# Moving the loads of batch 1's k and q, and their phi, among the steps of an attention-and-FFN kernel's first block

## The chip, the cores and the metric

The kernel runs on one core of a Trainium2 chip. The metric is device time in microseconds (us) of one execution; a "run" below is one execution. Traces are of one execution each, taken by the hardware profiler.

## The reference, cut to what matters

Cosine-weighted linear attention over 8 batches (8 heads, 576 positions, head width 64), then an RMS norm and a gated FFN (512 to 1536 to 512) on the 4608 tokens.

```python
def phi(x, c, s):                       # c, s: cosine and sine of the position
    r = np.maximum(x, 0.0)
    return np.concatenate([r * c, r * s], axis=-1)
q_p, k_p = phi(q, cos_w, sin_w), phi(k, cos_w, sin_w)
kv  = np.einsum('bhsf,bhsd->bhfd', k_p, v)
z   = np.sum(k_p, axis=2)
num = np.einsum('bhsf,bhfd->bhsd', q_p, kv)
den = np.einsum('bhsf,bhf->bhs', q_p, z)[..., None] + 1e-06
x   = num / den                         # then tokens by 512
xn  = x / rms(x) * rms_g
out = (silu(xn @ w_gate) * (xn @ w_val)) @ w_out
```

## The kernel before

The FFN goes block by block (512 tokens, one batch). A block has twelve gate steps, each with four matmuls by w_gate into a psG bank and four by w_val into a psV bank, and then the products with w_out. While PE (TensorE) works on a block's FFN, ACT (ScalarE) and DVE (VectorE) prepare the attention of the next batch. Each engine takes its own instructions in the order of the program, as every timeline here shows, so a wait holds up all that stands behind it (after the change, the sg of step 8, whose psG was ready near 34.3 us, ran at 36.98, behind two phis that had waited for k until 36.17). A bank is one of the buffers that PE writes its sums to; PE can fill it again only when ACT or DVE has read it. The order is written by hand:

```python
def phi(eng, out_ap, in_ap, scale):     # half of a phi: cosine on DVE, sine on ACT
    if eng is nc.scalar:
        nc.scalar.activation(out=out_ap, in_=in_ap, func=AF.Relu, scale=scale)
    else:
        eng.tensor_scalar(out=out_ap, in0=in_ap, scalar1=scale, scalar2=0.0,
                          op0=ALU.mult, op1=ALU.max)
# k_phi(eng, b, j, half) writes kpm from rk; q_phi(eng, b, c, half) writes qp from rq
...
def gval_step(blk, n, bank=None):
    bank = n % 2 if bank is None else bank       # two psG and two psV banks, taken in turn
    run(blk, n, "pe")
    gval_mm(blk, n, bank)                        # PE:  psG, psV
    run(blk, n, "pre")
    sg = gval_act(blk, n, bank)                  # ACT: sg = silu(psG)
    gval_h(blk, n, bank, sg)                     # DVE: hT = psV * sg
    run(blk, n, "post")                          # what at(blk, n, "post", ...) put there
...
# weight slices, issued from GpSimd (they cast to bf16), in this order:
#   0 to 5: w_gate and w_val, columns 0 to 768 in three pairs
#   6 w_gate, 7 w_val: columns 768 to 1152;  8 w_gate, 9 w_val: columns 1152 to 1536
#   then the first quarter of w_out
...
d = load_kv("k", 1)                              # issued from SP, as q and v
tc.add_manual_dep(d.ins, weight_dmas[7].ins.name, SYNC_DEP, reason="after the weights")
gate_q = load_q(1)
load_kv("v", 1, *LOW)
load_kv("v", 1, *HIGH)
w = wo_load(1)                                   # second quarter of w_out
tc.add_manual_dep(w.ins, gate_q.ins.name, SYNC_DEP, reason="after q of batch 1")
...
for j in range(NJ):                              # NJ = 9
    at(0, 8 + j // 4, "post", k_phi, V, 1, j, 0)
    at(0, 8 + j // 4, "post", k_phi, A, 1, j, 1)
for c in range(2):
    at(0, 10 + c, "post", q_phi, V, 1, c, 0)
    at(0, 10 + c, "post", q_phi, A, 1, c, 1)
...
for n in range(6, NNT):
    gval_step(0, n)                              # gate steps 6 to 11 of the first block
banks0 = [psC[0][:, :], psC[1][:, :], psG[0][:, :], psG[1][:, :]]
for n in range(NNT - 2):                         # w_out steps of the first block
    if n == 3:
        kvz_pe(1, psA)                           # "kvz": k_p^T [v, 1] of batch 1
        ...
    if 1 <= n <= 4:
        q_tr_pe(1, n - 1, qbank[n - 1])          # PE transposes q's phi, column n - 1
        ...
    if n == 0:
        for c in (2, 3):
            q_phi(V, 1, c, 0)
            q_phi(A, 1, c, 1)
    if n == 1:
        v_cast(A, 1, *LOW)
        v_cast(V, 1, *HIGH)
    ...
    for j in range(4):
        out_mm(0, j, n, banks0[j])
```

In the profile, L426 is gval_mm, L435 is sg, L441 is hT, L446 is out_mm, L209 is phi on ACT, L211 phi on DVE, L254 q_tr_pe, L282 kvz, L263 and L265 copies and casts on ACT and DVE, L79 and L90 the loads. rk, rq and rv are k, q and v as loaded; kpm and qp are what phi makes of k and q; vvm is v cast for kvz; rk<-in_k_dram is a load.

## Time and profile before

| | before |
|---|---|
| time | 328.86 us median (328.62 to 330.48, 3 runs) |
| span of the traced run | 327.9 us |
| PE busy | 318.9 us, 97% |
| PE's waits between gate step 6 and kvz | 0.25 and 1.03 us |

PE is the bound engine, so only its waits matter. First the part "busy us (share of the span) x instructions" of the page of the kernel before:

```profile
PE 318.9 (97%) x2441; PEld 161.0 (49%) x2441; DVE 185.9 (57%) x412; ACT 176.5 (54%) x366; POOL 32.1 (10%) x67
```

The timeline of PE before (start, length, engine, line, operation, what it writes and reads, count, and in brackets the idle time before it and who ended it):

```profile
39.64 1.02 PE L426 MATMUL psG<-xnT,wg 128*128 128x512 bf16 x4 [0.25 <-ACT sg L435]
...
43.20 0.38 PE L446 MATMUL psG<-wo,hT 128*128 128x512 bf16 x1 [1.03 <-ACT sg L435]
...
46.13 1.33 PE L282 MATMUL psA<-vvm,kpm 64*128 64x65 bf16 x72
```

PE waits for sg twice: gate step 11 wants the psG bank that the sg of step 9 has to empty, and the fourth w_out matmul wants the bank of step 11. The third line is kvz. ACT's timeline of the same stretch says why sg is late:

```profile
37.40 1.71 ACT L209 ACTIVATE kpm<-rk,tab 128x256 bf16<-128x256 f32 x4 [1.70 <-DMA rk<-in_k_dram]
39.01 0.57 ACT L435 ACTIVATE sg<-psG 128x512 f32<-128x512 f32 x1
39.49 1.69 ACT L209 ACTIVATE kpm<-rk,tab 128x256 bf16<-128x256 f32 x4
41.08 0.58 ACT L435 ACTIVATE sg<-psG 128x512 f32<-128x512 f32 x1
41.56 0.50 ACT L209 ACTIVATE kpm<-rk,tab 128x256 bf16<-128x256 f32 x1
41.96 0.71 ACT L209 ACTIVATE qp<-rq,tab 128x512 bf16<-128x512 f32 x1
42.57 0.58 ACT L435 ACTIVATE sg<-psG 128x512 f32<-128x512 f32 x1
```

ACT stands idle for 1.70 us until k has landed and then has no pause. SP's timeline has the issue of k, q and v:

```profile
27.46 0.38 SPq L79 DMA_DIRECT2D rk<-in_k_dram  x1
28.03 0.37 SPq L90 DMA_DIRECT2D rq<-in_q_dram  x1
28.57 5.19 SPq L79 DMA_DIRECT2D rv<-in_v_dram  x2
```

### The profile page before, as it was taken

To read this page: it belongs to the slowest core of one execution; us is meant where nothing else is said; L and a number is where in the kernel's file an instruction comes from. 1 tells how busy PE (TensorE), PEld (TensorE's weight loads), DVE (VectorE), ACT (ScalarE), POOL (GpSimd) and SP (SyncE) were. 2 spreads that over 40 slices of the span, in tenths; PEclk is the share of its full clock that TensorE was granted. 3 is DMA by queue.
4 is the path that set the end of the run, shared out by engine and by line. 5 is a ranking of instruction groups with operands and counts; after the bars stand their busy time and mean duration, and the time that the engine had idled before them with its cause. 6 is when DMAs were issued, how large, how long until landed. Compare 5 with 4: busy or idle time off the path is not lost.

```text
span 327.9 us, 6438 instructions
## 1 busy us (share of the span) xinstructions
PE 318.9 (97%) x2441; PEld 161.0 (49%) x2441; DVE 185.9 (57%) x412; ACT 176.5 (54%) x366; POOL 32.1 (10%) x67
## 2 busy tenths in 40 slices
PE   7999989999999999999999999999999999999994
PEld 2488455654445444544454445444544444444442
DVE  6775577777755875578257745773577133203310
ACT  6864575875566457645654576456644233223321
POOL 1660022001100110011001100110011000000000
PEclk9999999999999999999999999999999999999999
DMA  7999999998969866975598569957621400020014
GB/s 260 217 186 224 371 165 333 325 172 198 252 187 171 209 185 170 222 206 159 186 222 193 148 187 224 197 166 210 130 49 32 130 32 0 28 102 1 0 34 96
DMA packets 80337, 53.91 MB, mean 164 GB/s; under 512 B 51377, under 2 KB 67761, under 8 KB 80306
## 3 DMA queue, kind: packets, MB, share of 16 engines
q1 hardware_dynamic: 73264, 48.64, 57.8%
q0 software_dynamic: 6880, 4.72, 10.0%
q8 instruction: 19, 0.31, 0.4%
q10 hardware_dynamic: 162, 0.13, 0.2%
q14 instruction: 12, 0.10, 0.1%
HBM read 37.75 MB, written 9.44 MB: 144 GB/s over the span
## 4 chain that ended last, share of the span: by engine, by line
PE 83%; DMA 8%; ACT 4%; DVE 1%; issue 1%; SPq 1%; POOL 0%; ACTq 0%
PE psC L446 26%; PE psG L426 24%; PE psV L426 24%; DMA rk<-in_k_dram 3%; PE psA L282 3%; DMA wv<-in_moe_w_val_dram 3%; DMA rv<-in_v_dram 2%; PE psA L310 2%; ACT kpm L209 2%; PE psG L446 1%; ACT sg L435 1%; PE psC L826 1%; PE psV L254 1%; ACT qp L209 0%; PE psA L317 0%
## 5 line engine op out<-in xcount | busy, mean ns | idle before, releaser
L441 DVE TENSOR_TENSOR hT<-psV,sg 128x512 bf16<-128x512 f32 x102 | 70.3, 689 | 97.4 <-PE psV L426 84.9
L435 ACT ACTIVATE sg<-psG 128x512 f32<-128x512 f32 x102 | 60.6, 594 | 65.9 <-PE psG L426 65.8
L426 PE MATMUL psG<-xnT,wg 128*128 128x512 bf16 (+1 forms) x368 | 92.9, 375 | 0.3 <-ACT sg L435 0.2
L426 PE MATMUL psV<-xnT,wv 128*128 128x512 bf16 (+1 forms) x368 | 92.7, 374 | 0.0
L446 PE MATMUL psC<-wo,hT 128*128 128x512 bf16 x396 | 89.6, 379 | 0.0
L426 PEld LDWEIGHTS <-wv 128*128 128x128 bf16 x416 | 40.7, 98 | 47.4
L446 PEld LDWEIGHTS <-hT 128*128 128x128 bf16 x420 | 40.2, 98 | 46.4
L426 PEld LDWEIGHTS <-wg 128*128 128x128 bf16 x416 | 38.6, 98 | 41.7 <-issue 0.5
L263 ACT COPY osb<-psC 128x512 f32<-128x512 f32 (+1 forms) x33 | 19.2, 582 | 41.0 <-PE psC L446 39.7
L380 POOL TENSOR_TENSOR rs<-ms,mhalf 128x1 f32<-128x1 f32 x36 | 19.9, 551 | 200.2 <-ACT scr L375 200.2
L387 DVE SCALAR_TENSOR_TENSOR xn<-xt,rs,gb 128x512 bf16<-128x512 f32 x36 | 26.8, 745 | 14.7 <-POOL rs L380 14.7
L375 ACT ACTIVATE scr<-xt 128x513 bf16<-128x513 f32 x36 | 22.9, 635 | 21.4 <-DVE xt L364 21.2
L209 ACT ACTIVATE kpm<-rk,tab 128x256 bf16<-128x256 f32 (+1 forms) x78 | 31.8, 477 | 3.5 <-DMA rk<-in_k_dram 3.5
L364 DVE TENSOR_TENSOR xt<-psA,rec 128x512 f32<-128x512 f32 x35 | 24.2, 691 | 1.2
L211 DVE TENSOR_SCALAR kpm<-rk,tab 128x256 bf16<-128x256 f32 (+1 forms) x84 | 22.1, 329 | 3.0 <-DMA rk<-in_k_dram 3.0
L209 ACT ACTIVATE qp<-rq,tab 128x512 bf16<-128x512 f32 x32 | 22.5, 714 | 0.2 <-DMA rq<-in_q_dram 0.2
L211 DVE TENSOR_SCALAR qp<-rq,tab 128x512 bf16<-128x512 f32 x32 | 15.1, 484 | 0.5 <-DMA rq<-in_q_dram 0.5
L310 PEld LDWEIGHTS <-qpT 128*128 128x128 bf16 x248 | 11.6, 98 | 6.7 <-issue 0.3
L310 PE MATMUL psA<-kvzs,qpT 128*128 128x65 bf16 x248 | 12.8, 194 | 0.2
L426 PE MATMUL psV<-xnt_tail,wv 128*128 128x512 bf16 x48 | 12.3, 379 | 0.0
L426 PE MATMUL psG<-xnt_tail,wg 128*128 128x512 bf16 x48 | 12.3, 379 | 0.0
L282 PEld LDWEIGHTS <-kpm 64*128 64x128 bf16 x576 | 9.9, 95 | 3.8 <-issue 2.7
(89 smaller groups left out, 168.4 us busy)
## 6 DMA issues: line engine op xcount, KB each, us to landing
out_dram<-osb SPq DMA_DIRECT2D x32, 256.0 KB, 2.5
rv<-in_v_dram SPq DMA_DIRECT2D x21, 288.0 KB, 3.2
rk<-in_k_dram SPq DMA_DIRECT2D x20, 288.0 KB, 3.5
rq<-in_q_dram SPq DMA_DIRECT2D x20, 256.0 KB, 3.4
rk<-in_k_dram SPq DMA_DIRECT2D x2, 1152.0 KB, 8.8
rq<-in_q_dram SPq DMA_DIRECT2D x2, 1024.0 KB, 11.4
rv<-in_v_dram SPq DMA_DIRECT2D x3, 576.0 KB, 10.4
wo<-in_moe_w_out_dram POOLq DMA_DIRECT2D x4, 384.0 KB, 7.0
```

The costliest lines, as they stand in the source:

```text
L209: nc.scalar.activation(out=out_ap, in_=in_ap, func=AF.Relu, scale=scale)
L211: eng.tensor_scalar(out=out_ap, in0=in_ap, scalar1=scale, scalar2=0.0, op0=ALU.mult, op1=ALU.max)
L282: nc.tensor.matmul(banks[c][:, r * E : (r + 1) * E], lhsT=kp_main[b][lo : lo + 64, j, r, :], rhs=vvm[b % 2][lo : lo + 64, r, j, :], start= ...
L310: nc.tensor.matmul(o[:, g, i, :], lhsT=qpT[(b, 0)][:, h, j * P : (j + 1) * P], rhs=kvz_of(b, h), start=True, stop=True,)
L364: nc.vector.tensor_tensor(out=xt[:, 0:DM].rearrange("p (b h d) -> p b h d", b=2, d=D), in0=o[:, :, :, 0:D], in1=rec[:, :, :].unsqueeze(3). ...
L375: nc.scalar.activation(out=scr[:, :], in_=xt[:, 0 : DM + 1], func=AF.Square, scale=1.0 / math.sqrt(DM), accum_out=ms[:, :],)
L380: nc.gpsimd.tensor_tensor(out=rs[:, :], in0=ms[:, :], in1=mhalf[:, :], op=ALU.pow)
L387: nc.vector.scalar_tensor_tensor(out=xn[:, :], in0=x_of[(b, j)][:, 0:DM], scalar=rs_of[(b, j)][:, :], in1=gb[:, :], op0=ALU.mult, op1=ALU. ...
L426: nc.tensor.matmul(pst[bank][:, cols[0] : cols[1]], lhsT=w[:, t, n * P : (n + 1) * P], rhs=x[:, t, cols[0] : cols[1]], start=(t == 0), sto ...
L435: nc.scalar.activation(out=sg[:, :], in_=psG[bank][:, :], func=AF.Silu)
L441: nc.vector.tensor_tensor(out=hTs[blk][:, n, :], in0=psV[bank][:, :], in1=sg[:, :], op=ALU.mult)
L446: nc.tensor.matmul(bank, lhsT=hTs[blk][:, n, j * P : (j + 1) * P], rhs=wo[:, n, :], start=(n == 0), stop=(n == NNT - 1),)
```

## The change

Its intent: k arrives earlier, ahead of the last weight slices, and its phi comes in twos instead of fours, so that sg is never far behind. q goes behind the last gate slice so that it does not compete with it. The whole change:

```diff
     d = load_kv("k", 1)
-    tc.add_manual_dep(d.ins, weight_dmas[7].ins.name, SYNC_DEP, reason="after the weights")
+    tc.add_manual_dep(d.ins, weight_dmas[6].ins.name, SYNC_DEP, reason="after most weights")
     gate_q = load_q(1)
+    tc.add_manual_dep(
+        gate_q.ins, weight_dmas[8].ins.name, SYNC_DEP, reason="after the gate weights"
+    )
 ...
     for j in range(NJ):
-        at(0, 8 + j // 4, "post", k_phi, V, 1, j, 0)
-        at(0, 8 + j // 4, "post", k_phi, A, 1, j, 1)
-    for c in range(2):
-        at(0, 10 + c, "post", q_phi, V, 1, c, 0)
-        at(0, 10 + c, "post", q_phi, A, 1, c, 1)
+        at(0, 7 + j // 2, "post", k_phi, V, 1, j, 0)
+        at(0, 7 + j // 2, "post", k_phi, A, 1, j, 1)
+    at(0, 11, "post", q_phi, V, 1, 0, 0)
+    at(0, 11, "post", q_phi, A, 1, 0, 1)
 ...
         if n == 0:
-            for c in (2, 3):
+            for c in (1, 2, 3):
                 q_phi(V, 1, c, 0)
                 q_phi(A, 1, c, 1)
```

No instruction is added or taken away.

## The prediction

> **What bounds the kernel.** TensorE: the page gives PE busy for 318.9 of 327.9 us (97%), at full granted clock. In the waits view PE's named waits sum to under 5 us, and two of them lie where the change acts, both on ACT's Silu (sg): 0.25 us at 39.6 us (gate step 11) and 1.03 us at 43.2 us (a w_out matmul that takes over the bank of step 11). ACT's timeline has the cause. k of batch 1 is issued at 27.46 us, when weight slice 7 lands, and lands at 37.4. ACT, in program order, waits 1.70 us for it, then does phi four at a time (1.7 us) ahead of the sg of steps 10 and 11. So at most 1.28 us (0.4%) is to be had.
>
> **What changes.** No instruction is added or removed; PE's order is the same. k waits for one slice less: by the landings it is issued near 25.5 us. q waits for the last gate slice (landed 29.4 before), so near 29.6 instead of 28.03; v queues behind it.
>
> **DMA.** By the packets, k first flowed at 31.0 us, 3.5 us after its issue (1.1 us at the start of the kernel); until then the weights alone wrote about 200 GB/s. From 31.0 both flowed, weights at 100 and k at 200, which agrees with the round robin that the Trainium skill describes (DMA: Bandwidth & Descriptors, Queues, rings and completion order). Estimate from these: k flows from about 29 us and, at 200 GB/s for 1.18 MB, lands near 35 (34 to 36). The last weight slice slips from 31.2 to about 33; PE wants it at 36.6. q follows k without a gap and lands near 39.8 (40.2 before), v near 42 and 43.5.
>
> **After.** ACT reaches the first phi behind the sg of step 7, at 34.0, and waits about 1 us. Then two phis (0.9 us) and one sg (0.5 us) fit each 1.73 us step, so ACT catches up by step 10, and the sg of step 11 ends near 40.9, before PE wants the bank (41.8). Both waits go: 1.28 us. Some may be handed back: three q phis and the cast of v now stand directly before kvz on an ACT without slack (cast ends near 44.9, when PE arrives): 0 to 0.4 us. w_out's second part, still issued after q (landed 45.8), is wanted at about 46.3: 0 to 0.3 us. Later stages only shift.
>
> **Predicted:** 328.86 - 1.3 + 0.2 = 327.8 us, range 326.9 to 329.0. Faster by over 2%: 0.01; within 2%: 0.98; slower by over 2%: 0.01.
>
> **What would show it.** Right: k's packets start near 29 us; ACT waits for rk at 34, about 1 us; PE's waits at 39.6 and 43.2 are gone; kvz of batch 1 (46.2 before) starts near 45; block 2's first gate step (92.8) and the end move as much. Wrong: a new PE wait of step 10 or 11 on sg (k landed after 36), on qp or vvm before kvz, or on w_out.
>
> **What would make it wrong.** k getting no bandwidth until the weights end: then ACT, blocked two steps earlier, holds up the sg of step 8, PE waits at step 10, and nothing is gained or up to 1 us lost. Or k slowing the weight slices of steps 9 to 11 past 36 us. Or q late, and w_out after it. None of these is near 2%.

## The result, and the profile after

| | median of 6 runs | lowest to highest |
|---|---|---|
| before | 328.78 us | 328.62 to 330.48 |
| changed | 329.03 us | 328.67 to 329.64 |

The ratio is 1.000, 95% interval 0.9978 to 1.0022. Ratios here are the mean time of one kernel's fast runs over that of the other's in the same rounds, so they are not quite the ratio of the medians quoted. The change neither gained nor lost anything that these runs can show.

The page of the changed kernel has PE as busy as before:

```profile
PE 318.6 (97%) x2441; PEld 161.0 (49%) x2441; DVE 186.1 (57%) x412; ACT 176.2 (54%) x366; POOL 31.9 (10%) x67
```

The timeline of PE after:

```profile
37.60 1.02 PE L426 MATMUL psG<-xnT,wg 128*128 128x512 bf16 x4 [0.61 <-ACT sg L435]
...
43.01 0.61 PE L254 MATMUL psV<-ident,qp 128*128 128x128 bf16 x8 [0.93 <-ACT qp L209]
...
45.72 1.33 PE L282 MATMUL psA<-vvm,kpm 64*128 64x65 bf16 x72
```

Both old waits are gone, and two new ones stand in their place: 0.61 us at gate step 10 for an sg, and 0.93 us in front of the first transpose of q's phi. ACT's timeline after:

```profile
36.17 0.91 ACT L209 ACTIVATE kpm<-rk,tab 128x256 bf16<-128x256 f32 x2 [2.85 <-DMA rk<-in_k_dram]
36.98 0.57 ACT L435 ACTIVATE sg<-psG 128x512 f32<-128x512 f32 x1
37.45 0.89 ACT L209 ACTIVATE kpm<-rk,tab 128x256 bf16<-128x256 f32 x2
...
40.80 0.59 ACT L435 ACTIVATE sg<-psG 128x512 f32<-128x512 f32 x1
41.28 0.51 ACT L209 ACTIVATE kpm<-rk,tab 128x256 bf16<-128x256 f32 x1
41.68 2.56 ACT L209 ACTIVATE qp<-rq,tab 128x512 bf16<-128x512 f32 x4
```

ACT now comes to the first phi one gate step earlier, waits 2.85 us for k instead of 1.70, and the sg of step 8 is what it holds up. DVE's timeline just before the first transpose:

```profile
41.42 0.69 DVE L441 TENSOR_TENSOR hT<-psV,sg 128x512 bf16<-128x512 f32 x1
42.03 0.44 DVE L211 TENSOR_SCALAR kpm<-rk,tab 128x256 bf16<-128x256 f32 x1
42.39 1.66 DVE L211 TENSOR_SCALAR qp<-rq,tab 128x512 bf16<-128x512 f32 x4
```

The product of step 11, k's last phi and only then q's first one (four in a row, a little over 0.4 us each): it is done at 42.86 us, and PE starts at 43.01. PE had been ready since about 42.1 (43.01 less 0.93). The view puts this wait down to ACT, whose second phi of q ended at 43.01. It was DVE: the first transpose reads only q's first phi, of which ACT's half was done at 42.40, and its weight load (PEld, here the timeline of 42.6 to 43.3 us) began at 42.98, before ACT's second phi ended:

```profile
42.98 0.41 PEld L254 LDWEIGHTS <-qp 128*128 128x128 bf16 x7 [1.39 <-ACT qp L209]
```

In all five traces with this wait PE started 0.14 to 0.15 us after DVE's phi had ended, and three of the five views name DVE.

k was issued at 25.39 us:

```profile
25.39 0.38 SPq L79 DMA_DIRECT2D rk<-in_k_dram  x1
29.41 0.37 SPq L90 DMA_DIRECT2D rq<-in_q_dram  x1
29.95 3.71 SPq L79 DMA_DIRECT2D rv<-in_v_dram  x2
```

The DMA queues in the window of 29 to 33 us (queue, kind, packets, MB written, share of 16 engines), first before, then after; q0 carries the weights, q1 carries k:

```profile
q0 software_dynamic: 690, 0.60, 92.2%
q1 hardware_dynamic: 176, 0.41, 28.9%
```

```profile
q1 hardware_dynamic: 366, 0.84, 60.4%
q0 software_dynamic: 389, 0.35, 52.9%
```

After, the two queues moved about as many packets each (366 and 389), which agrees with the round robin by packets that the Trainium skill describes ("DMA: Bandwidth & Descriptors", Queues, rings and completion order). k's packets are the larger ones (2304 bytes against 768 or 1024), so k got more than two thirds of the bytes.

### The profile page after: what moved, and what is told of

It is laid out like the page before. It is cut to its first block, busy times and chain, and to the rows that moved or that the text cites. A ratio compares the mean times of both kernels' runs of the same rounds, so it can differ in the third digit from the quotient of the medians.

```text
span 327.5 us, 6440 instructions
## 1 busy us (share of the span) xinstructions
PE 318.6 (97%) x2441; PEld 161.0 (49%) x2441; DVE 186.1 (57%) x412; ACT 176.2 (54%) x366; POOL 31.9 (10%) x67
## 4 chain that ended last, share of the span: by engine, by line
PE 83%; DMA 8%; ACT 4%; DVE 1%; issue 1%; SPq 0%; ACTq 0%; POOL 0%
PE psC L446 26%; PE psG L426 25%; PE psV L426 24%; DMA rk<-in_k_dram 3%; PE psA L282 3%; DMA wg<-in_moe_w_gate_dram 3%; DMA rv<-in_v_dram 2%; PE psA L310 2%; ACT kpm L209 2%; PE psG L446 1%; ACT sg L435 1%; ACT qp L209 1%; PE psV L254 1%; PE psC L828 1%; PE psA L317 0%
```

## The experiments

**How to compare traces.** The first 30 us differ from run to run: PE's first matmul of gate step 6 came between 29.78 and 31.36 us in the thirteen traces, as much as the whole effect. So times below marked "+" count from that matmul. kvz is the first matmul of batch 1's kvz; all that comes behind it is the same work (kvz to block 2's first gate step took 46.64 to 46.65 us in twelve of the traces, 46.86 in e10). PE's listed waits run short: the view gives a single 512-column matmul 0.38 us, though in an unbroken row they start 0.22 us apart. So a listed wait behind one stands for about 0.16 us more, and a delay under about 0.3 us is not listed (before: 1.28 us listed, and kvz 1.60 us behind that of e5, which has no wait).

The theories that the first runs were to separate:

- *Main theory at that time*: ACT works in program order, so all hangs on when the whole of k has landed. k landed at 36.14 us, not 35, and ACT was made to wait for it one step earlier.
- *Rival 1*: the loads cost. q, issued later, makes its phi late, or the slowed weights make PE wait.
- *Rival 2*: the new places of phi cost, and the loads gain.

Four kernels ran together, with 11 runs of the kernel before on the same chip (median 328.66 us).

### e1: the new loads alone

```diff
 # against the kernel before
-    tc.add_manual_dep(d.ins, weight_dmas[7].ins.name, SYNC_DEP, reason="after the weights")
+    tc.add_manual_dep(d.ins, weight_dmas[6].ins.name, SYNC_DEP, reason="after most weights")
     gate_q = load_q(1)
+    tc.add_manual_dep(gate_q.ins, weight_dmas[8].ins.name, SYNC_DEP, ...)
```

> The new loads with the old places of phi. All times count from PE's first matmul of gate step 6 (kvz of batch 1 came 15.54 us after it before, 15.80 after the change). Main theory (the time hangs on when ALL of k has landed, and on ACT working off a queue behind it in program order): k lands near +6.2 as after the change, ACT is blocked one step later than after the change, so PE has no wait at step 10; the old wait for the bank of step 11 stays at 0.9 to 1.1 us; kvz near +15.3; time 0.1 to 0.3 us under before. Rival 1 (the loads themselves cost: q issued later, weights slowed): kvz at or past +15.8 with new PE waits on weights or q. Rival 2 (the spread of phi costs and the loads gain): all of the 1.28 us gone, kvz near +14.5.

Measured: 328.01 us (6 runs), ratio 0.9985 (0.9971 to 0.9999). In its trace k landed at +3.85, PE has no listed wait, and kvz came at +13.94. The expected k at +6.2 was a miss: the same loads that brought k at +6.22 in the trace of the changed kernel brought it at +3.85 here. By its kvz this run supports rival 2. By its time it stands between the two: 0.65 us under before in the medians, where the main theory said 0.1 to 0.3 and e2's text asks more than 1 of rival 2.

### e2: the new places of phi alone

```diff
 # against the changed kernel
-    tc.add_manual_dep(d.ins, weight_dmas[6].ins.name, SYNC_DEP, reason="after most weights")
+    tc.add_manual_dep(d.ins, weight_dmas[7].ins.name, SYNC_DEP, reason="after the weights")
     gate_q = load_q(1)
-    tc.add_manual_dep(gate_q.ins, weight_dmas[8].ins.name, SYNC_DEP, ...)
```

> The old loads with the new places of phi. Main theory: k lands near +6.8, ACT stands blocked in step 7 from +3.3, so PE waits about 1.2 us at step 10 and about 1.2 us for q's phi in front of its first transpose; kvz near +16.4, time 0.8 us over before. Rival 1 (the loads cost, the spread gains): kvz before +15.5, time under before. Rival 2 (the spread costs): time over before as well, but then e1 must gain more than 1 us.

Measured: 329.65 us (6 runs), ratio 1.0037 (1.0023 to 1.0052): slower, clear of noise. k landed at +6.43 and kvz came at +16.02. The waits of PE:

```profile
37.81 1.02 PE L426 MATMUL psG<-xnT,wg 128*128 128x512 bf16 x4 [0.82 <-ACT sg L435]
...
43.23 0.61 PE L254 MATMUL psV<-ident,qp 128*128 128x128 bf16 x8 [0.94 <-ACT qp L209]
```

Both are the waits of the changed kernel, a little larger at step 10, and under the 1.2 us each that had been expected. So the new places cost, and rival 1, by which they should have gained, does not hold here.

### e3: the changed kernel with k one slice earlier

```diff
 # against the changed kernel
-    tc.add_manual_dep(d.ins, weight_dmas[6].ins.name, SYNC_DEP, ...)
+    tc.add_manual_dep(d.ins, weight_dmas[5].ins.name, SYNC_DEP, ...)
```

> The changed kernel with k issued one weight slice earlier still (after slice 5). Main theory: k lands near +4.3, two steps ahead of the first sg it could hold up, so the 0.61 us wait at step 10 goes; the wait of about 0.9 us for q's phi stays, because DVE makes it only behind the product of step 11, whatever k does; kvz near +14.8, time 0.7 us under before. Rival 1 (loads cost): the weight slices of steps 9 to 11 slip behind PE's use, with PE waits on weights, and kvz stays past +15.5. A third possibility: the qp wait goes as well (then it was backlog from k alone), kvz near +14.2.

Measured: 328.72 us (6 runs), ratio 1.0004 (0.9991 to 1.0017). k landed at +2.15, two us before the expected +4.3. The wait at step 10 is gone; the one in front of the transpose is not, and kvz came at +14.94:

```profile
42.12 0.61 PE L254 MATMUL psV<-ident,qp 128*128 128x128 bf16 x8 [0.84 <-DVE qp L211]
```

DVE's timeline in front of it, in which DVE was not behind (0.23 us idle before the product):

```profile
40.52 0.69 DVE L441 TENSOR_TENSOR hT<-psV,sg 128x512 bf16<-128x512 f32 x1 [0.23 <-PE psV L426]
41.13 0.35 DVE L211 TENSOR_SCALAR kpm<-rk,tab 128x256 bf16<-128x256 f32 x1
41.39 1.76 DVE L211 TENSOR_SCALAR qp<-rq,tab 128x512 bf16<-128x512 f32 x4
```

With k far ahead of need, 0.84 us of wait remain, as the order on DVE alone would have it. The traced kvz came as expected; the expected 0.7 us of time did not show in the timed runs.

### e4: q without its wait for the gate slice

```diff
-    tc.add_manual_dep(
-        gate_q.ins, weight_dmas[8].ins.name, SYNC_DEP, reason="after the gate weights"
-    )
```

> The changed kernel without q's wait for the last gate slice, so q is issued right behind k. Main theory: nothing changes: k lands within 0.4 us of +6.2, q was not what its phi waited for (it had landed at +9.5, ACT took it up at +11.8), waits of 0.6 and 0.9 us stay, kvz at +15.8 within 0.3. Rival 1 (q's later issue costs): the qp wait falls by half or more and kvz comes before +15.3.

Measured: 329.19 us (4 runs), ratio 1.0013 (0.9995 to 1.0031). q landed at +8.52 (+9.54 in the changed kernel), and the wait for its phi was 0.89 us all the same. k landed at +5.58, kvz at +15.12, with a gap of only about 0.1 us at step 10. That kvz is before the +15.3 at which rival 1 was to be believed, but k landed 0.64 us earlier than in the changed kernel, the wait for qp hardly fell, and the time is no better. q's later issue is not where the time went, and no trace has a PE wait on a weight; rival 1 falls.

The theory was therefore put in two parts. *(a)* A late k holds up the sg behind it. *(b)* The new places put q's first phi behind step 11's product on DVE, which costs PE 0.8 to 0.9 us in front of its first transpose whatever k does. Part (b) is rival 2, made precise. Four more kernels ran together (before: 328.65 us, 11 runs).

### e5: k early, phi in its old places

```diff
 # against the kernel before
-    tc.add_manual_dep(d.ins, weight_dmas[7].ins.name, SYNC_DEP, reason="after the weights")
+    tc.add_manual_dep(d.ins, weight_dmas[5].ins.name, SYNC_DEP, reason="after most weights")
     gate_q = load_q(1)
+    tc.add_manual_dep(gate_q.ins, weight_dmas[8].ins.name, SYNC_DEP, ...)
```

> k issued after weight slice 5, q after the last gate slice, and phi in its old places (q's first phi ahead of step 11's product). The theory after the first four runs has two parts: (a) a late k holds up sg behind it, (b) the spread moved q's first phi behind step 11's product on DVE, which costs PE 0.8 to 0.9 us in front of its first transpose whatever k does. By it k lands near +2.2 to +4, no PE wait between +0 and kvz, kvz at +13.9 to +14.1, time 0.8 to 1.5 us under before (ratio 0.9955 to 0.9975), steadier than e1, whose k can land late. If instead e1 gained by chance of its run, and the early k costs by slowing the weights, kvz comes past +14.9.

Measured: 327.69 us (327.12 to 327.83, 6 runs), ratio 0.9958 (0.9933 to 0.9984). k landed at +2.68; the waits view lists nothing for PE between 25 and 64 us; kvz at +13.94. PE's first transpose and kvz, neither with a wait:

```profile
41.20 0.61 PE L254 MATMUL psV<-ident,qp 128*128 128x128 bf16 x8
...
43.91 1.33 PE L282 MATMUL psA<-vvm,kpm 64*128 64x65 bf16 x72
```

All as expected. The last weight slice landed at +4.12, before step 9's w_val matmuls (about +6.0) read it; no weight was late.

### e6: e3 with one DVE instruction moved

```diff
-    at(0, 11, "post", q_phi, V, 1, 0, 0)
+    at(0, 10, "post", q_phi, V, 1, 0, 0)
```

> e3 with one instruction moved: DVE's half of q's first phi stands ahead of step 11's product, ACT's half stays behind its sg. Part (b) of the theory: PE's 0.84 us wait in front of the first transpose falls to 0.0 to 0.2 us, kvz at +14.0 to +14.3 (e3: +14.94), time 0.6 us under e3. If the wait comes from ACT's half or from q's landing, it stays above 0.5 us.

Measured: 328.03 us (6 runs), ratio 0.9977 (0.995 to 1.0003). kvz came at +14.24 instead of e3's +14.94, and the waits view has no PE wait before kvz. DVE and PE:

```profile
41.47 0.73 DVE L211 TENSOR_SCALAR qp<-rq,tab 128x512 bf16<-128x512 f32 x1
42.13 0.67 DVE L441 TENSOR_TENSOR hT<-psV,sg 128x512 bf16<-128x512 f32 x1
```

```profile
42.63 0.62 PE L254 MATMUL psV<-ident,qp 128*128 128x128 bf16 x8
```

Moving that one instruction took the wait away. kvz is still 0.30 us behind e5's, almost all of it in two delays too short for the view: 0.13 us in front of this transpose, which now waits for ACT's half of the phi (done at 42.58), and 0.15 us in front of kvz, which waits for ACT's cast of v (done at 45.46, kvz at 45.51). Part (b) is shown in the trace; the times of e3 and e6 come from different calls, and their intervals overlap, so the times alone do not show it.

### e7: the changed kernel with both halves of q's first phi in the old place

```diff
-    at(0, 11, "post", q_phi, V, 1, 0, 0)
-    at(0, 11, "post", q_phi, A, 1, 0, 1)
+    at(0, 10, "post", q_phi, V, 1, 0, 0)
+    at(0, 10, "post", q_phi, A, 1, 0, 1)
```

> The changed kernel with both halves of q's first phi ahead of step 11. Part (b): the wait for qp goes. Part (a) stays as k's landing has it: with k at +6.2, 0.6 us at step 10, and up to 0.4 us for the bank of step 11 or for the cast of v, kvz near +15.3; with k at or under +4.5 no wait, kvz near +14.0. Time 0.3 to 0.8 us under the changed kernel.

Measured: 327.71 us (6 runs), ratio 0.9967 (0.9941 to 0.9994). k landed at +4.09, no wait, kvz at +13.95. Beside e8, the changed kernel in the same rounds, this is 1.11 us less in the medians (0.92 in the means) for two moved instructions, more than the 0.3 to 0.8 expected.

### e8: the changed kernel again

> The changed kernel unchanged, for a second trace. The theory: k's landing differs from run to run (with these loads it was +3.9 to +6.2 in three traces), as one or a few of the 16 engines lag; the wait at step 10 follows it (none if k is in by about +5.5, 0.6 at +6.2), while the wait for qp is 0.8 to 1.0 us in any case. Time as before, ratio 0.999 to 1.001.

Measured: 328.82 us (6 runs), ratio 0.9995 (0.9971 to 1.0019). In this trace k landed at +3.32. The wait at step 10 is gone, the one for q's phi stayed, and kvz came at +14.84:

```profile
43.14 0.61 PE L254 MATMUL psV<-ident,qp 128*128 128x128 bf16 x8 [0.74 <-DVE qp L211]
```

So the 0.61 us of the first trace belong to k's landing in that run, and the other wait belongs to the order.

A last call asked for a second trace of before, and whether spreading k's phi is worth something by itself (before: 328.73 us, 11 runs).

### b2: the kernel before again

> The kernel before, unchanged, for a second trace: the first one was of an execution 0.9 us over the median. The theory: k lands between +5.5 and +6.8 and the wait for the bank of step 11 follows it one for one; with k earlier than in the first trace, kvz comes earlier by as much (+14.6 to +15.6). Ratio 0.998 to 1.002.

Measured: 328.66 us (4 runs), ratio 0.9998 (0.9979 to 1.0018). k landed at +5.99, 0.80 us earlier than in the first trace (+6.79), and kvz came at +14.75, 0.79 us earlier: one for one. PE's only wait there:

```profile
41.80 0.38 PE L446 MATMUL psG<-wo,hT 128*128 128x512 bf16 x1 [0.65 <-ACT sg L435]
```

The first trace of before was thus of a run with a late k.

### e9: k early, phi spread, q's first phi in its old place

```diff
 # against e7
-    tc.add_manual_dep(d.ins, weight_dmas[6].ins.name, SYNC_DEP, reason="after most weights")
+    tc.add_manual_dep(d.ins, weight_dmas[5].ins.name, SYNC_DEP, reason="after most weights")
```

> k after slice 5, k's phi spread over steps 7 to 11, both halves of q's first phi ahead of step 11. The theory: once k is early and q's first phi in its old place, the spread is worth nothing either way: no PE wait, kvz at +13.9 to +14.0, ratio within 0.002 of e5 in the same rounds. If spreading helps in itself, it is under e5 by more than 0.5 us.

### e10: e5 again

> e5 again, beside e9 and for a second interval: kvz at +13.9 to +14.0, ratio 0.995 to 0.998.

Measured: e9 327.84 us (6 runs), ratio 0.9974 (0.9959 to 0.999); e10 327.65 us (8 runs), ratio 0.9962 (0.9946 to 0.9978). e10's kvz came at +13.94 as expected. e9's came at +14.45, a miss of half a microsecond. In this run q landed at +9.89; q's first phi stood on ACT in front of the sg of step 11 and waited for it, and the cast of v, further back on ACT, was late for kvz. ACT, then PE:

```profile
39.73 0.72 ACT L209 ACTIVATE qp<-rq,tab 128x512 bf16<-128x512 f32 x1 [0.56 <-DMA rq<-in_q_dram]
```

```profile
44.27 1.33 PE L282 MATMUL psA<-vvm,kpm 64*128 64x65 bf16 x72 [0.29 <-ACT vvm L263]
```

The old place of q's first phi has its own risk, then: it must not stand where q has not yet landed. In time e9 and e10 cannot be told apart (ratios 0.0012 apart); spreading k's phi showed no gain of its own once k was early.

### All traces side by side

"All landed" is when the last of the 16 completion counts of k's load arrived (one for each DMA engine), "first" the first of them; PE waits are those that the view lists between step 6 and kvz.

| run | k waits for slice | places of phi | k first / all landed | PE waits, us | kvz |
|---|---|---|---|---|---|
| before | 7 | old | +4.44 / +6.79 | 0.25, 1.03 (sg) | +15.54 |
| b2 | 7 | old | +4.19 / +5.99 | 0.65 (sg) | +14.75 |
| e1 | 6 | old | +3.38 / +3.85 | none | +13.94 |
| e5 | 5 | old | +2.20 / +2.68 | none | +13.94 |
| e10 | 5 | old | +1.07 / +1.82 | none | +13.94 |
| e2 | 7 | new | +4.52 / +6.43 | 0.82 (sg), 0.94 (qp) | +16.02 |
| changed | 6 | new | +4.34 / +6.22 | 0.61 (sg), 0.93 (qp) | +15.80 |
| e4 | 6 | new | +3.66 / +5.58 | 0.89 (qp) | +15.12 |
| e8 | 6 | new | +2.83 / +3.32 | 0.74 (qp) | +14.84 |
| e3 | 5 | new | +1.34 / +2.15 | 0.84 (qp) | +14.94 |
| e6 | 5 | new, DVE's half of q's first phi old | +1.07 / +1.89 | none | +14.24 |
| e7 | 6 | new, q's first phi old | +3.65 / +4.09 | none | +13.95 |
| e9 | 5 | new, q's first phi old | +2.37 / +3.00 | 0.29 (vvm) | +14.45 |

Two lines fit the rows with purely old or new places. Where k is late, kvz follows its landing: 8.75 and 8.76 us behind it with the old places (before, b2), 9.54 to 9.59 us with the new ones (e4, changed, e2). Where k is early, kvz stands at +13.94 with the old places and at +14.84 to +14.94 with the new ones. On either line the new places cost 0.8 to 1.0 us. The wait at step 10 grows one for one with k's landing in the two traces that list it: 0.61 at +6.22, 0.82 at +6.43. No trace has a late k with the phi of k spread and q's first phi in its old place, so what that move is worth with a late k is not shown.

## Why the prediction was right or wrong

The measured ratio of 1.000 is within 2%, as forecast at 0.98; that says little, since a gain of 1 us (0.3%) and none at all both lie there. The predicted gain of about 1 us did not come: 327.8 was forecast, and the median was 329.03, just past the upper end of the stated range (329.0), beside a median of before of 328.78 in the same table.

- **What bounds the kernel, and the two waits: right**, and both waits went (a slip of wording: the first group of four phis stood ahead of the sg of step 9, not 10). But their size was read from one trace of a run with a late k. The second trace of before had 0.65 us of listed wait instead of 1.28, and kvz 0.81 us behind that of e5 instead of 1.60. So "at most 1.28 us" was no bound: the waits of that trace were worth more, those of the other less.
- **k's packets near 29 us: right**, 28.98. The last weight slice was forecast near 33 and landed at 33.72; q near 39.8, and it landed at 39.46. No weight and no q was waited for.
- **"lands near 35 (34 to 36)": wrong in size in the traced run.** The first of the 16 counts of k's load came at 34.26 us and the fifteenth at 35.19, near the estimate from the mean rate, but the last came at 36.14. The Trainium skill says that only the full count means that all data has landed ("DMA: Bandwidth & Descriptors", Why a DMA increments its semaphore by 16 and not by 1), and this trace shows the price: 1.88 us between the first count and the last. The estimate divided bytes by a rate, and so had the finish of the average engine instead of the slowest one. ACT waited 2.85 us instead of about 1, and PE 0.61 us at step 10. With k issued after the same slice it landed at 33.92 us in e1, 33.87 in e7, 34.34 in e8 and 36.73 in e4, so the landing differs from run to run by more than the stated range, and one trace does not size it. In e8 that wait was absent. The text named this case ("k landed after 36") without giving it much weight.
- **"Some may be handed back ... 0 to 0.4 us": the step that failed.** It followed ACT alone. The wait came from DVE, where the change had put q's first phi behind step 11's product and k's last phi; as listed it measured 0.74 to 0.94 us in five traces with the new places (0.93, 0.94, 0.84, 0.89, 0.74). e6 removed it by moving one DVE instruction. A wait "on qp or vvm before kvz" stands among the prediction's own signs of being wrong, but its reckoning had no term for DVE. On ACT alone e6 shows about 0.3 us (0.13 and 0.15), inside its 0 to 0.4. The transposes need both halves of a phi, so both engines' orders had to be followed.
- **w_out handed back 0 to 0.3 us: no such wait** was listed in any trace.

Taken together: the change's own loads gained 0.65 us in the medians (e1; 1.0 us in e5, with k one slice earlier still), and the new places gave it back (e2: 1.0 us over before). With q's first phi left in its old place the change gains 0.94 us (e7), near the predicted 1.1.

What stays open: timed runs have no trace, so how often k lands late in them is not known. That may be why traced gaps (1.6 us between e5 and the first trace of before) are larger than timed ones (1.0 us), and why e3 with a kvz at +14.94 timed no better than before; neither is shown. Whether e5 is faster than e1 is not shown either: their intervals overlap, and kvz is at +13.94 in both. And no view says which DMA engines lag.

## What to carry to other kernels

When work is moved to another place in hand-ordered code, follow each engine's own order from the moved instruction to the next PE instruction that reads it; here one phi slipped behind one product on DVE and cost as much as an earlier load had gained. Plan with the landing of the slowest DMA engine rather than with bytes over rate (36.14 against 35 us here), and with more than one trace. A version that beats both kernels is e5: k loaded after weight slice 5, q after the last gate slice, and all phis left where they were (ratios to before 0.9958 and 0.9962, a gain of 0.4%; 327.69 us beside 328.82 us of the changed kernel in the same rounds, e8).

## What the Trainium skill lacked or had wrong

- "DMA: Bandwidth & Descriptors", Latency and other measured facts, gives about 600 ns to the first byte on the SP path. With quiet queues this agrees if one counts from the end of the issuing instruction: the first k load's was issued at 0.74 us, took 0.46 us, and the first packet started at 1.84, 0.64 us behind its end. With the weight queue busy, the first packet of batch 1's k started 3.57 to 3.65 us after the start of its issue in all thirteen traces. The page has no first-byte figure for a busy queue; the cause of the 3.6 us was not found.
- The same page says that a load completes when all its engines have counted, but has no figure for how far they spread. Between first and last count of the same 1.18 MB load it was 0.44 us (e7) to 2.34 us (before).
- "Perfetto Trace Analysis", Optimizing Scalar/DVE Operations, says that breaking up instructions may help where ACT or DVE cause bubbles without being saturated. No instruction was broken up here, so this is not tested; groups of four phis were only spread into twos. That gained nothing measurable once k was early (e9 0.9974, e10 0.9962), and where it moved one phi behind a product PE waited 0.74 to 0.94 us. The page does not speak of an engine's program order as the thing to check.
- "TensorE: Matmul & The Clock Gate", Part 1, says that the warm-up differs from run to run and is not worth fitting, at under 1% of a usual span. In e4, e6, e8 and e10 the clock, granted in full from 5.6 to 6.0 us on, fell back to half for one stretch of 3.41 us near 9 us, and gate step 6 started at 31.02 to 31.36 us, against 29.78 to 30.59 in the other nine. The page's window of about 3.4 us agrees, and so does the 1%; but an effect of 1 us (0.3%) is of the same size, and times have to be counted from behind it.
